# Half of the last stores issued from ScalarE's queue, with new due times for the planned order

## The chip, the cores and the metric

The kernel runs on one core of a Trainium2 chip. A core has a matrix engine (TensorE, PE in the profile), a vector engine (VectorE, DVE), a scalar engine for functions by table (ScalarE, ACT), GpSimd (POOL) and a sync engine (SyncE, SP), which here only issues DMAs. Each engine works through its own instructions in order; semaphores hold an instruction until what it needs is there. The metric is the device time of one execution in microseconds (us), the median of several runs.

## The reference, cut to what matters

The input u is 2048 positions by 512 channels. It is normalised, and the normalised xn goes two ways: through a long convolution whose kernel K comes from a state-space model with 128 states per channel, and through a mixing block with an MLP (512 to 1376 to 512).

```python
def reference(u, A_re, A_im, B_re, B_im, C_re, C_im, log_dt, Dskip, w1, w2, w3, w4):
    xn = layernorm(u)
    # K[d, l] = Re sum_n C[d, n] * exp(dt * A[d, n] * l) * dt * B[d, n]
    K = einsum("dn,dnl,dn->dl", C, exp(dt * A[:, :, None] * l), dt * B).real
    s = irfft(rfft(xn, 2L) * rfft(K, 2L))[:L] + xn * Dskip      # causal convolution
    h = gelu(layernorm(xn) @ w1)
    hs = shift_quarters(h, (+1, -1, +2, -2)) @ w2               # four channel quarters shifted in position
    x1 = xn + hs
    b = x1 + gelu(layernorm(x1) @ w3) @ w4
    return u + s * silu(b)
```

## The kernel before, in words

Positions lie on the 128 partitions in four quarters r of 32, with 16 slabs s of 512 channels; X, of 128 x 16 x 512, holds xn, then x1, then b, then the result. The convolution is done by hand-written Fourier steps as matrix products: u_stage1 transforms xn, tables(0) and tables(1) make K for two channel halves (phases, sines, cosines and exponentials on ScalarE and VectorE, sums on TensorE), kstage1 transforms K, products multiplies the spectra and starts the way back, and inverse ends it. The results of the stages go through DRAM (scr_Ud, scr_Kfa, scr_Zda and the like). mlp(g), for eight groups g of two slabs, is the largest part of TensorE's work: for each of six column blocks jp, 24 products into pb (fewer in the last block), a GELU on ScalarE, a split into two f16 parts (ghl), and 12 products into pa.

The end of the kernel, on which the change bears, is this. gate(g) applies SiLU to two slabs of X once mlp(g) is done. inverse(hf, g) (lines 898 to 911) loads zin from scr_Zda (hf = 0, the first 256 channels) or scr_Zdb (hf = 1, the second 256), does 8 small products per slab (pc or pd), and VectorE multiplies them into X. finish_first(g) (line 914) adds u to the first half of two slabs (the tile xh) and stores it; finish(g) (line 924) adds u to the second half (the tile xr, loaded for two groups at once) and stores it. A store goes by by_r (line 581): one DMA of 32 partitions, 64 KB, for each of the four quarters r. So each of the 16 calls issues four stores, 64 in all, and all of them from SP, which also issues every load and every store of the kernel.

The program order is not the order of execution. Every instruction is first put down in a Plan (line 147) with its dependencies, a cost, and a due time vt. Plan.order (line 253) then walks through time: it takes the engine that can start first, and of the operations that are ready there the one with the smallest vt. For an operation that ScalarE or VectorE may do (class Either), whichever engine comes first by these rules takes it, with a penalty added to vt (PREFER and AVOID, or PREFERP and AVOIDP where the source is in PSUM); a change of ScalarE's function table adds SWITCH. Operations on SP have a cost of 0.45 us, and their data lands later by a rate and the constant LAND. Each engine's instructions are then issued in that order. The vt of a step is set by due (line 575): a base, worked out from constants such as H0, MC, FA or FB, plus one entry of SHIFT for each of 361 calls. All instructions are issued from line 313, so the profile shows that line for nearly everything, and groups are told apart by the names of their tiles.

Of the kernel before, what the change touches and what calls it, by code (L numbers as in the profile page):

```python
# [83 lines left out]
class Op:  # L84
# [10 lines left out]
SAME = {"PE": 0.0, "ACT": 0.13, "DVE": 0.1, "SP": 0.0}  # L95
TABLE_LOAD = 1.41
DMA_RATE = 300e3
LAND, PAD = 2.65, 0.16
BASE, FINE, END = 16512, 19840, 229368

KGC, QUAD = 3.25, 0.95
WARM = 40

SHIFT = (
# [24 lines left out]
)  # L129
Q0, QC = -3744.9, 0.33  # L130
SWITCH = 12134.9
PREFERP, AVOIDP = 8082.45, -17238.7
PREFER, AVOID = 17860.0, 18183.0
PV, T0, TC = 1856.7, 239.9, 2383.42
LX, LC, LP, LW, LV = -4000.0, 0.08, -3071.8, 12710.4, 25366.6
M0, MC, WC = 1389.9, 9549.57, 0.4
H0, HC, SC = 4574.5, 2.54, 0.26
KA, PA, PAC, FA = -2867.9, -39190.2, 0.07, 17550.1
KB, PB, PBC, FB = 5280.7, 10111.3, 0.23, -6058.6
FC = 0.08  # L140


def mlp_due(g, jp):
# [3 lines left out]
class Plan:  # L147
# [105 lines left out]
    def order(self):  # L253
# [17 lines left out]
        while len(out) < len(ops):  # L271
# [4 lines left out]
            for o in pools[e]:  # L276
                if o.ready <= t + 0.02:
                    v = o.vt
                    if e == "ACT" and o.table and o.table != table:
                        v += SWITCH  # L280
                    if len(o.alts) > 1:
# [37 lines left out]
def is_ap(x):  # L319
    return hasattr(x, "tensor") and hasattr(x, "ap")  # L320


def columns(ap):
    n = 1
    for s in ap.shape[1:]:
        n *= s
    return n


def pe_cost(name, args):  # L330
    f = 1 if args[2].dtype == F16 else 4
    return 0.11 if name == "transpose" else columns(args[2]) * f / 2400.0 + 0.0025 * (1 + f // 4)


def act_cost(args, kw):
    small = sum(1 for k in ("bias", "scale") if is_ap(kw.get(k)))
    cost = columns(args[0]) * (0.00075 if "PSUM" in str(args[1].space) else 0.00084) + 0.092 + 0.088 * small
    return cost + (0.11 if is_ap(kw.get("accum_out")) else 0.0)


def dve_cost(name, args):
    aps = [a for a in args if is_ap(a)]
    n = columns(aps[0])
    small = sum(1 for a in aps[1:] if columns(a) == 1 and n > 1)
    if name == "bn_aggr":
        return 0.095
    if name == "reciprocal":
        return 0.07 + n * 0.0064
    if name == "memset":
        return 0.06 + n * 0.0003  # L350
    if name in ("bn_stats", "tensor_reduce"):
        return 0.045 + columns(aps[1]) / 960.0
    if name in ("tensor_scalar", "tensor_copy") and "PSUM" not in str(aps[1].space):
        return 0.068 + n * 0.00052 + 0.052 * small
    return 0.065 + n / 960.0 + 0.06 * small


class Engine:
# [3 lines left out]
    def __getattr__(self, name):  # L362
        def call(*args, **kw):
            aps = [a for a in args if is_ap(a)] + [kw[k] for k in ("bias", "scale") if is_ap(kw.get(k))]
            writes, reads = aps[:1], aps[1:]
            if is_ap(kw.get("accum_out")):
                writes = writes + [kw["accum_out"]]
            if name == "matmul" and not kw["start"]:
                reads = reads + writes
            table, nbytes = 0, 0  # L370
            if self.eng == "PE":
                cost = pe_cost(name, args)
            elif self.eng == "ACT":
                cost = act_cost(args, kw)
                if name == "activation":
                    table = TABLES.get(args[2], 0)
            elif self.eng == "DVE":
                cost = dve_cost(name, args)
            else:
                cost = 0.45  # L380
                nbytes = 4 * min(columns(a) * a.shape[0] for a in aps)
            self.plan.add({self.eng: (cost, (name, args, kw))}, writes, reads, table, nbytes)

        return call
# [38 lines left out]
def kernel(  # L423
# [9 lines left out]
    V, A, T, Q = [Engine(plan, e) for e in ("DVE", "ACT", "PE", "SP")]  # L433
# [3 lines left out]
    ov = out[0].rearrange("(t r s) d -> r t s d", r=4, s=S)  # L437
# [5 lines left out]
    DH = D // 2  # L443
# [13 lines left out]
    def at(offset, shape, dt, name):  # L457
        return nc.alloc_sbuf_tensor_at(name, shape, dt, offset=offset)[:]
# [116 lines left out]
    def due(t=None):  # L575
        plan.stage += 1
        t = plan.base = plan.base if t is None else t
        plan.vt = t + (SHIFT[plan.stage] if plan.stage < len(SHIFT) else 0)


    def by_r(sb, dr, to_dram=False):

        for r in range(4):
            a, d = sb[32 * r : 32 * r + 32], dr[r]
            Q.dma_start(d, a) if to_dram else Q.dma_start(a, d)

    w1s, w2s = [], []

# [304 lines left out]
    def gate(g):  # L893
        due(FA + FC * g)
        X2 = X[:, 2 * g : 2 * g + 2]
        A.activation(X2, X2, AF.Silu)

    def inverse(hf, g):
        due((FA, FB)[hf] + FC * g)
        ch = slice(hf * DH, hf * DH + DH)  # L900
# [13 lines left out]
    def finish_first(g):  # L914
        due(FA + FC * g)
        x = xhr([P, 2, DH], F32, "xh")
        by_r(x, xv[:, :, 2 * g : 2 * g + 2, :DH])
        X2 = X[:, 2 * g : 2 * g + 2, :DH]
        V.tensor_add(X2, X2, x)
        by_r(X2, ov[:, :, 2 * g : 2 * g + 2, :DH], to_dram=True)  # L920
# [3 lines left out]
    def finish(g):  # L924
        due(FB + FC * g)
        if g % 2 == 0:
            xr.append(at(xrs.pop(), [P, 4, DH], F32, "xr"))
            by_r(xr[-1], xv[:, :, 2 * g : 2 * g + 4, DH:])
        X2 = X[:, 2 * g : 2 * g + 2, DH:]
        V.tensor_add(X2, X2, xr[-1][:, 2 * (g % 2) : 2 * (g % 2) + 2])  # L930
        by_r(X2, ov[:, :, 2 * g : 2 * g + 2, DH:], to_dram=True)


    def pow2_scale(cols, dst_s, dst_inv, target):
# [301 lines left out]
    for g in range(8):  # L1236
        finish(g)
# [27 lines left out]
```

## Time and profile before

| | us |
|---|---|
| runs shown | 679.21, 679.72, 677.94 |
| median | 679.21 |
| profiled execution, its own time | 675.68 |
| its span, first to last instruction | 673.9 |
| mean granted TensorE clock | 0.969 |
| TensorE products busy | 629.6 |
| VectorE busy | 538.8 |
| ScalarE busy | 477.3 |
| 64 stores of the output, first issue to end of the last | 635.40 to 671.50 |

The profile shows one execution. Its engines are listed with their busy time; SPq is the queue of DMAs that SP issues, and the duration of a row there is that of the issue, not of the transfer. A row of the groups ends with the idle time of the engine just before it and what that time waited for. In the order of time each row has its start and its duration in us from the span's start.

### The profile page before, as it was taken

What the parts mean: (1) busy time and instruction counts of PE and PEld (TensorE: products, weight loads), DVE (VectorE), ACT (ScalarE), POOL (GpSimd) and SP (SyncE); (2) the same over time, 40 slices, a digit from 0 to 9 for tenths busy, and PEclk for the clock granted to TensorE, in tenths of its full rate; (3) what the DMA queues carried; (4) which work ended last, traced back from release to release, by engine and by line L of the source; (5) the groups of instructions that cost most, each with busy time, mean ns of one, the idle gap of its engine ahead of it and who ended that gap; (6) DMA issues with size and microseconds to landing.
All of it is one profiled execution on the core that took longest, in us unless ns stands there. A gap on an engine that the chain in (4) does not pass through costs nothing.

```text
span 673.9 us, 13919 instructions
## 1 busy us (share of the span) xinstructions
PE 629.6 (93%) x5526; PEld 417.0 (62%) x5526; DVE 538.8 (80%) x798; ACT 477.3 (71%) x1051; POOL 0.7 (0%) x6
## 2 busy tenths in 40 slices
PE   7799899999996998998999999999999999999972
PEld 7567667475465786565677576677555854567520
DVE  5899899999999999988999999987533247454472
ACT  3999899978877999896999996984534335242420
POOL 0000000000000000000000000000000000000000
PEclk9899979999998999998999999999999999999995
DMA  8945351511112110486233333343988778747954
GB/s 244 232 154 187 107 196 57 199 49 48 63 48 79 43 50 28 101 211 182 74 110 116 89 120 116 103 142 111 242 218 252 182 181 231 189 138 206 311 144 125
DMA packets 108432, 95.61 MB, mean 142 GB/s; under 512 B 49680, under 2 KB 90640, under 8 KB 107984
## 3 DMA queue, kind: packets, MB, share of 16 engines
q1 hardware_dynamic: 108368, 94.74, 49.8%
q8 instruction: 43, 0.70, 0.4%
q14 instruction: 21, 0.17, 0.1%
HBM read 61.16 MB, written 33.55 MB: 141 GB/s over the span
## 4 chain that ended last, share of the span: by engine, by line
PE 45%; DVE 36%; ACT 5%; DMA 5%; issue 4%; SPq 3%; DVEq 0%; ACTq 0%
PE pb L313 18%; DVE pt L313 11%; PE pa L313 10%; PE pc L313 9%; PE pd L313 8%; DVE kt L313 6%; DVE X L313 3%; SPq L313 3%; DVE pr L313 3%; DMA X<-in_A_u_dram 2%; DVE stats L313 2%; DVE eg L313 2%; ACT mag L313 2%; DVE ghl L313 2%; DVE pab L313 2%
## 5 line engine op out<-in xcount | busy, mean ns | idle before, releaser
L313 PE MATMUL pb<-x1T,w3h 128*128 128x256 f16 (+1 forms) x1056 | 125.2, 275 | 1.9 <-DVE w3h L313 1.0
L313 PE MATMUL pa<-w4h,ghl 128*128 128x512 f16 (+1 forms) x528 | 124.5, 384 | 1.2 <-DVE w4h L313 0.8
L313 PEld LDWEIGHTS <-w3h 128*128 128x128 f16 (+1 forms) x1056 | 102.6, 101 | 29.9 <-issue 15.2
L313 ACT ACT_TABLE_LOAD x78 | 100.1, 1283 | 2.4 <-PEq L1253 0.7
L313 PEld LDWEIGHTS <-ghl 128*128 128x128 f16 (+1 forms) x528 | 49.3, 99 | 67.8 <-issue 17.4
L313 ACT ACTIVATE mag<-par 128x64 f32<-128x64 f32 x512 | 85.2, 275 | 4.6 <-DVE kt L313 2.8
L313 PE MATMUL pc<-kt 128*32 128x64 f32 x1024 | 83.9, 417 | 0.6 <-DVE kt L313 0.6
L313 PE MATMUL pc<-pt 128*32 128x64 f32 x1024 | 77.6, 388 | 0.0
L313 PE MATMUL pb<-xT,w 128*128 128x256 f32 x256 | 61.3, 396 | 1.7 <-ACT hT L313 1.7
L313 PEld LDWEIGHTS pb<-xT,w 128*128 128x128 f32 x256 | 49.7, 198 | 14.2 <-issue 4.0
L313 PEld LDWEIGHTS pc<-pt 128*32 128x32 f32 x1024 | 55.9, 195 | 0.0
L313 ACT ACTIVATE g<-pb,wsc 128x512 f32<-128x512 f32 (+1 forms) x48 | 32.4, 690 | 32.5 <-PE pb L313 32.1
L313 PEld LDWEIGHTS pc<-kt 128*32 128x32 f32 x1024 | 48.3, 176 | 10.4 <-issue 7.5
L313 DVE SCALAR_TENSOR_TENSOR ghl<-g,wsc,ghl 128x512 f16<-128x512 f32 (+1 forms) x48 | 35.1, 739 | 24.4 <-ACT ghl L313 24.3
L313 DVE TENSOR_TENSOR kt<-mag,kt 128x1024 f32<-128x1024 f32 x32 | 42.8, 1336 | 0.3 <-ACT mag L313 0.3
L313 ACT ACTIVATE ghl<-g,wsc 128x512 f16<-128x512 f32 (+1 forms) x33 | 23.3, 710 | 24.6 <-PE pa L313 23.6
L313 DVE TENSOR_TENSOR pr<-pc,kh 128x512 f32<-128x512 f32 x32 | 21.0, 686 | 23.5 <-PE pc L313 17.1
L313 DVE SCALAR_TENSOR_TENSOR pt<-kt,pt 128x2080 f32<-128x2080 f32 x16 | 39.5, 2472 | 0.1
L313 PE MATMUL pd<-pr,cst 64*128 64x256 f32 x256 | 36.3, 402 | 1.1 <-DVE pr L313 1.1
L313 ACT COPY z1e<-pd 128x256 f32<-128x256 f32 x45 | 15.3, 383 | 29.2 <-PE pd L313 28.9
L313 ACT ACTIVATE kt<-kt,halfpi 128x2080 f32<-128x2080 f32 x16 | 32.3, 2020 | 0.0
L313 ACT ACTIVATE pt<-pt 128x2080 f32<-128x2080 f32 x16 | 31.3, 1959 | 0.1
(160 smaller groups left out, 970.3 us busy)
## 6 DMA issues: line engine op xcount, KB each, us to landing
wst<-in_B_w_dram SPq DMA_DIRECT2D x20, 512.0 KB, 3.7
scr_Ud<-ue SPq DMA_DIRECT2D x16, 512.0 KB, 3.2
scr_Kfa<-k1e SPq DMA_DIRECT2D x16, 256.0 KB, 3.5
uin<-scr_Ud SPq DMA_DIRECT2D x32, 128.0 KB, 2.9
cst<-c_gp SPq DMA_DIRECT2D x16, 256.0 KB, 2.8
kin<-scr_Kfa SPq DMA_DIRECT2D x32, 128.0 KB, 2.7
scr_Zda<-z1e SPq DMA_DIRECT2D x16, 256.0 KB, 2.7
cst<-c_gp SPq DMA_DIRECT2D x8, 512.0 KB, 4.2
```

Source lines behind the costliest of these rows:

```text
L313: ins = [getattr(self.engines[op.eng], name)(*args, **kw).ins for name, args, kw in op.calls]
```

## The change

Two edits of the code, and new numbers. by_r takes a pair of queues and uses them in turn for stores; finish passes SP's and ScalarE's, so that quarters 0 and 2 of each second half are stored from SP and quarters 1 and 3 from ScalarE. finish_first still stores from SP alone, and all loads stay on SP. The planner counts 0.45 us for a DMA on ScalarE. All 361 entries of SHIFT, the constants of the bases, the penalties and LAND (2.65 to 2.66) are replaced, so the planned order changes throughout.

```diff
-LAND, PAD = 2.65, 0.16
+LAND, PAD = 2.66, 0.16
 SHIFT = (
...
 )
-Q0, QC = -3744.9, 0.33
-SWITCH = 12134.9
-PREFERP, AVOIDP = 8082.45, -17238.7
-PREFER, AVOID = 17860.0, 18183.0
-PV, T0, TC = 1856.7, 239.9, 2383.42
-LX, LC, LP, LW, LV = -4000.0, 0.08, -3071.8, 12710.4, 25366.6
-M0, MC, WC = 1389.9, 9549.57, 0.4
-H0, HC, SC = 4574.5, 2.54, 0.26
-KA, PA, PAC, FA = -2867.9, -39190.2, 0.07, 17550.1
-KB, PB, PBC, FB = 5280.7, 10111.3, 0.23, -6058.6
-FC = 0.08
+Q0, QC = -11967.6, 0.09
+SWITCH = 10650.5
+PREFERP, AVOIDP = 13121.6, -24212.5
+PREFER, AVOID = 25936.6, 18011.2
+PV, T0, TC = 6435.1, 7692.7, 2695.8
+LX, LC, LP, LW, LV = -4000.0, 0.48, -17943.2, -1849.6, 49755.3
+M0, MC, WC = 10270.3, 8551.58, 0.66
+H0, HC, SC = 12245.0, 0.07, 0.14
+KA, PA, PAC, FA = -19279.1, -38345.8, 0.43, 41121.5
+KB, PB, PBC, FB = 3161.8, 3594.7, 0.05, -41595.5
+FC = 0.06
...
             elif self.eng == "ACT":
-                cost = act_cost(args, kw)
+                cost = 0.45 if name == "dma_start" else act_cost(args, kw)
...
-    def by_r(sb, dr, to_dram=False):
+    def by_r(sb, dr, to_dram=False, queues=(Q, Q)):
 
         for r in range(4):
             a, d = sb[32 * r : 32 * r + 32], dr[r]
-            Q.dma_start(d, a) if to_dram else Q.dma_start(a, d)
+            queues[r % 2].dma_start(d, a) if to_dram else Q.dma_start(a, d)
...
-        by_r(X2, ov[:, :, 2 * g : 2 * g + 2, DH:], to_dram=True)
+        by_r(X2, ov[:, :, 2 * g : 2 * g + 2, DH:], to_dram=True, queues=(Q, A))
```

49 rows, old and new, of the table SHIFT are left out of this document.

## The prediction

> **What bounds the kernel now.** I read the page first, then busy times in five stretches, then the order of time and the chain of waits over the last 40 us, then the groups of that tail and of the middle.
>
> ```profile
> span 673.9 us, 13919 instructions
> PE 629.6 (93%) x5526; PEld 417.0 (62%) x5526; DVE 538.8 (80%) x798; ACT 477.3 (71%) x1051; POOL 0.7 (0%) x6
> PEclk9899979999998999998999999999999999999995
> ```
>
> TensorE is busy for 629.6 of 673.9 us, so 44 us are to be had at most without touching its work. The next view, whose columns are the stretch, its length, the busy time of each engine, the granted clock, the DMA share and GB/s, says where they lie.
>
> ```profile
> 0.00:40.00 40.00, 31.64 (x171) 26.59 (x172) 29.79 (x98) 26.51 (x79) 0.70 (x6) 0.91 0.94 245
> 40.00:120.00 80.00, 75.25 (x604) 57.62 (x603) 76.55 (x95) 76.37 (x182) 0.00 (x0) 0.96 0.40 132
> 120.00:400.00 280.00, 266.66 (x2454) 175.08 (x2455) 274.47 (x345) 249.12 (x565) 0.00 (x0) 0.98 0.32 93
> 400.00:650.00 250.00, 248.64 (x2207) 155.67 (x2204) 146.26 (x240) 124.26 (x227) 0.00 (x0) 1.00 0.67 184
> 650.00:674.00 24.00, 7.44 (x99) 2.08 (x97) 11.76 (x25) 1.06 (x1) 0.00 (x0) 0.63 0.49 126
> ```
>
> TensorE idles 8.4 us in the loads at the start, 4.8 us up to 120, 13.3 us from 120 to 400, 1.4 us from 400 to 650, and 16.6 us behind 650. From 120 to 400 VectorE is busy for 98% of the time and is the bound; from 400 to 650 TensorE is. Behind 650 no compute engine is: even VectorE works for only half of it. What ends last there is seen in the order of time (start, duration, engine, operation).
>
> ```profile
> 611.71 0.69 DVE L313 TENSOR_TENSOR X<-X,xh 128x512 f32<-128x512 f32 x1
> ...
> 628.04 0.69 DVE L313 TENSOR_TENSOR X<-X,xh 128x512 f32<-128x512 f32 x1
> ...
> 635.40 36.09 SPq L313 DMA_DIRECT2D out_dram<-X  x64
> ...
> 646.75 0.69 DVE L313 TENSOR_TENSOR X<-X,xr 128x512 f32<-128x512 f32 x1
> ...
> 648.50 0.66 PE L313 MATMUL pd<-zin,is 64*32 64x256 f32 x16
> ...
> 649.10 1.47 PE L313 MATMUL pa<-w4h,ghl 96*128 96x512 f16 x6
> ...
> 652.75 1.06 ACT L313 ACTIVATE X<-X 128x1024 f32<-128x1024 f32 x1 [8.04 <-DVE X L313]
> ...
> 660.60 1.43 PE L313 MATMUL pc<-zin,is 64*32 64x256 f32 x16 [0.56 <-DVE X L313]
> ...
> 660.91 0.69 DVE L313 TENSOR_TENSOR X<-X,xr 128x512 f32<-128x512 f32 x1
> ...
> 662.90 0.69 DVE L313 TENSOR_TENSOR X<-X,xr 128x512 f32<-128x512 f32 x1
> 670.58 0.92 SPq L313 DMA_DIRECT2D out_dram<-X  x2
> ```
>
> The last addition, which finishes the output, ends at 662.90 + 0.69 = 663.59. SP issues its last two stores until 670.58 + 0.92 = 671.50, and the span ends 2.4 us later. So for 7.9 us everything is computed and SP alone works off a queue. The chain of waits names the same thing (start, duration, what).
>
> ```profile
> 643.36 0.43 SPq L313
> 643.79 0.04 issue
> 643.83 0.44 SPq L313
> ...
> 648.16 1.59 SPq L313
> 649.75 0.04 issue
> 649.79 0.43 SPq L313
> ```
>
> One store costs 0.43 to 0.44 us and a gap of 0.04, 0.48 in all, and from 643.36 SP no longer waits for data. One issue took 1.59, 1.15 more than the others. (671.50 - 643.36 - 1.15) / 0.48 = 56, so 56 of the 64 stores stand in that train. They stand there because they were late: six additions of the first halves (the rows from 611.71 to 628.04) were done before the first store left at 635.40, so 24 stores were waiting already.
>
> **The change part by part.** *The stores.* Of the 64 stores, the 32 of the second halves are split: rows r = 1 and 3 of each group go to ScalarE's queue, two of the four, so 16 leave SP. The 32 of the first halves stay on SP.
>
> ```profile
> L313 DVE TENSOR_TENSOR X<-X,xr 128x512 f32<-128x512 f32 x8 | 5.5, 690 | 0.2
> L313 DVE TENSOR_TENSOR X<-X,xh 128x512 f32<-128x512 f32 x2 | 1.4, 686 | 0.0
> L313 DVE TENSOR_TENSOR X<-X,pc 128x256 f32<-128x256 f32 x10 | 3.8, 417 | 1.6 <-PE pc L313 1.5
> L313 PE MATMUL pc<-zin,is 64*32 64x256 f32 x80 | 6.0, 534 | 4.0 <-DVE X L313 4.0
> L313 PE MATMUL pd<-zin,is 64*32 64x256 f32 x64 | 3.0, 385 | 0.6 <-DVE X L313 0.6
> ```
>
> These groups are of the time after 644. All eight additions of second halves (xr) fall there, so all 16 stores that leave SP leave the train. In the old order SP would then hold 56 - 16 = 40 stores: 643.36 + 40 x 0.48 + 1.15 = 663.7. But the last group's two SP stores can't start before its addition ends: 663.59 + 0.05 + 2 x 0.48 = 664.6. That is the later of the two, so it holds. The gain is 671.50 - 664.6 = 6.9 us.
>
> What of it lies on ScalarE: 16 issues by 0.48 are 7.7 us. ScalarE's last work is the SiLU at 652.75, behind 8.04 us of idling, and nothing follows until 673.9; that is the cover. Queued behind a store that waits for its addition there is only this SiLU of the last slabs, and further stores; without the cover (stores ahead of a GELU of the last matrix products) each group of two would hold ScalarE for up to one period of the additions, 2.0 us between the last ones. The price of a store on ScalarE's queue isn't in this trace. The nearest rows are the same stores on SP:
>
> ```profile
> L313 SPq DMA_DIRECT2D out_dram<-X x64: 315/431/1864, 635.4 to 671.1; - x64
> DMA to landing us min/median/max: 1.7/1.7/5.5
> ```
>
> At the least, 0.32 us, ScalarE is through before SP and nothing changes. At the most, 1.86 us, 16 stores take 29.8 us, and from the first possible one (647.4, the end of the first second-half addition) ScalarE would issue until 677.2: 5.7 us worse than before. I take 0.48, the median with its gap, since the transfer is the same one.
>
> Would the transfers keep up? These rows are of the stretch before the train is alone, and of the train's end:
>
> ```profile
> 620.00:650.00 30.00, 30.00 (x267) 15.97 (x264) 14.40 (x27) 10.83 (x14) 0.00 (x0) 1.00 0.89 251
> 664.00:674.00 10.00, 0.00 (x0) 0.00 (x0) 0.00 (x0) 0.00 (x0) 0.00 (x0) 0.50 0.45 115
> ```
>
> 56 stores of 65.5 KB in 21.2 us (643.4 to 664.6) are 173 GB/s, where 251 have been moved. There is room.
>
> *The due times.* Every SHIFT and nearly every base changes, so the whole order does, though no instruction beside table loads is added or removed. In planning units the new values look like the old ones stretched by about half, with noise. Two readings of them: the second halves' steps now start from -41,595 and the first halves' from 41,122 (before: -6,059 and 17,550), so where both are ready the second halves go first, and the very last stores may be those that SP issues alone (four by 0.48, so 1.0 us later than in my sum). The penalty that keeps a free choice off VectorE rises from 17,860 to 25,937, that for ScalarE falls a little. Bounds of the reordering: all idle time of 120 to 400 gained, -13.3 us; as much again lost, +13.3. No row speaks for a sign, so I take 0.
>
> *The sum.* 673.9 - 6.9 = 667.0 span. The profiled execution took 675.68, 1.8 around its span, so 668.8 for such a run. The median of the runs, 679.21 (677.94 to 679.72), lies 3.5 above the profiled one; I keep that distance: 679.21 - 6.9 = 672.3.
>
> **The rivals.**
>
> *The tail shrinks further (668.9).* Once SP isn't last, the inverse steps are. After 644 there are nine of them (80 and 64 products, 16 in each), six of them behind the last matrix products of 649.10; at a clock of 0.63 one takes up to 1.43 us, where that at 648.50 took 0.66. If five of them go ahead of the last matrix products, those end 5 x 0.66 = 3.3 later, at 653.9. Then follow the two slabs' updates and the SiLU (3.2, as from 650.57 to 653.81), four multiplications by 0.417 and two additions by 0.69 (3.1), two stores (1.0) and 2.4: 663.6 span, 3.4 below my sum. For it speaks the dip of the clock in the last slice; against it that the 24 waiting stores must then leave before 635, or SP (663.7 + 2.4 = 666.1) is the bound again.
>
> *The two queues take turns (679.2).* The trace has no second queue, so it can't exclude that issuing is one resource. If a part t of each 0.48 is exclusive, the train ends at 643.36 + 56 t + 1.15, which passes 664.6 from t = 0.36 on; at t = 0.48 nothing is gained. For it: the shortest issue took 0.32, close to that point. Against it: the usual 0.43 stands for one queue alone, where the sequencer's own work is included.
> The Trainium skill, Perfetto Trace Analysis, section "DMA Instruction — HWDGE (DVE, Sync)", says that the descriptor generator is locked for one instruction while its descriptors are made, and that the sequencers share it; by that rule this rival has its place. The Trainium skill, DMA: Bandwidth & Descriptors, section "Issuing engines are not separate DMA queues", says that issuing on several engines saves just the sequencer's time to start a transfer; by that rule the full 6.9 stands, because here it is this time that is queued, and no run so far shows which page decides.
>
> *ScalarE overruns the middle (685.4): slower.* The rows are of 120 to 400.
>
> ```profile
> L313 DVE TENSOR_SCALAR kt<-pt 128x2080 f32<-128x2080 f32 (+1 forms) x9 | 12.1, 1346 | 0.1
> L313 ACT ACTIVATE kt<-pt,magic 128x2080 f32<-128x2080 f32 x5 | 10.1, 2022 | 1.7 <-DVE pt L313 1.6
> L313 ACT ACT_TABLE_LOAD x44 | 56.5, 1283 | 1.1 <-PE pb L313 0.4
> ```
>
> Nine phase steps that either engine may take run on VectorE at 1.35 us; on ScalarE the like takes 2.02. With the new penalties all nine may move: 18.2 us more on ScalarE, of whose 280 us 30.9 are free. The cost of changing its table falls from 12,135 to 10,651, so there may also be more table loads, at 1.28 each; ten fill what is left. From 17 more on (18.2 + 21.8 - 30.9 = 9.1) the loss passes the gain of 6.9 and the 2.0 us of a measurable difference; at 20 it is 13.0, and the time 679.2 - 6.9 + 13.0, 685.3 to 685.4. For it: 44 loads in 280 us are many already, and ScalarE is 89% busy. Against it: VectorE, the bound there, would be relieved by 12 us at the same time.
>
> *Part is given back (677).* The same stretch loses 3 to 7 us without a single cause.
>
> **How the numbers follow.** What a measurement of this kernel can tell from no change is about 0.3%, 2.0 us. My forecast, the stores' gain with an order that is worth the same, has 0.50 (its own range 669 to 675.5); the shorter tail 0.20; part given back 0.10, half of it within 2 us of the old time; the queues taking turns 0.06; the overrun 0.14. Faster: 0.50 + 0.20 + 0.05 = 0.75; the same: 0.05 + 0.06 = 0.11; slower: 0.14. The range 666.5 to 680.5 leaves out the overrun and the best of the shorter tails; it takes in half of the reordering's gain and no more than the old time with a little on top.
>
> **What would show it.** Right, if the profile after has 16 stores on ScalarE's queue and 48 on SP's, the last SP issue ends within about 1.5 us of the last addition instead of 7.9 behind it, the stores on ScalarE take 0.3 to 0.6 us, and the stretch behind the last matrix product falls from 23 to about 16 us. The queues take turns if issues on both stretch to 0.8 us and more where they overlap. The overrun shows as more than 60 table loads between 120 and 400 and as ScalarE busy throughout a stretch in which TensorE idles. Wrong I am if TensorE's idle time between 40 and 650, 19.5 us now, changes by more than 5 us either way, or if the span's end is set by something else than a store.

## The result and the profile after

The changed kernel takes 673.88 us (median of four runs, 672.62 to 674.53), where the kernel before took 678.92 beside it (677.94 to 679.72). The ratio is 0.9924, with a 95% interval of 0.9904 to 0.9944. Measured again later, beside the kernel before, it was 675.31 against 679.36 (0.9941, 0.9913 to 0.9968). So it is 4 to 5 us faster. The forecast was 672.3. The way there is another one than forecast, as the rest shows.

The first lines of the profile after: the span, the engines' busy time and the granted clock.

```profile
span 672.1 us, 13936 instructions
PE 630.7 (94%) x5526; PEld 418.5 (62%) x5526; DVE 535.1 (80%) x788; ACT 479.2 (71%) x1060; POOL 0.7 (0%) x6
PEclk9889979999997998999999999999999999999995
```

The span is 1.8 us shorter, and the profiled execution took 673.90. Its stretches, with the columns of the table before (stretch, length, the engines, clock, DMA share, GB/s):

```profile
0.00:40.00 40.00, 31.13 (x167) 26.20 (x168) 30.31 (x100) 26.37 (x79) 0.70 (x6) 0.87 0.90 242
40.00:120.00 80.00, 75.86 (x610) 58.98 (x609) 75.57 (x92) 76.90 (x184) 0.00 (x0) 0.96 0.40 133
120.00:400.00 280.00, 266.58 (x2422) 175.52 (x2421) 275.29 (x341) 254.35 (x596) 0.00 (x0) 0.97 0.33 94
400.00:650.00 250.00, 249.21 (x2238) 155.62 (x2236) 142.56 (x235) 120.51 (x204) 0.00 (x0) 1.00 0.65 183
650.00:674.00 24.00, 7.94 (x96) 2.15 (x96) 11.38 (x24) 1.06 (x1) 0.00 (x0) 0.61 0.51 133
```

Up to 650 the two kernels look alike: TensorE idles 4.1 + 13.4 + 0.8 = 18.4 us between 40 and 650, where it was 19.5. What is new stands in the tail. First the stores by queue (shortest, median and longest issue in ns; first and last start):

```profile
L314 SPq DMA_DIRECT2D out_dram<-X x48: 315/426/1961, 633.2 to 669.3; - x48
L314 ACTq DMA_DIRECT2D out_dram<-X x16: 322/437/460, 647.7 to 664.1; - x16
...
DMA to landing us min/median/max: 1.6/1.7/5.0
```

Then the order of time of the tail (start, duration, engine, operation):

```profile
643.50 26.24 SPq L314 DMA_DIRECT2D out_dram<-X  x36
...
646.08 2.77 PE L314 MATMUL pa<-w4h,ghl 128*128 128x512 f16 x12
...
647.02 0.69 DVE L314 TENSOR_TENSOR X<-X,xr 128x512 f32<-128x512 f32 x1
647.75 0.87 ACTq L314 DMA_DIRECT2D out_dram<-X  x2
...
652.96 11.57 ACTq L314 DMA_DIRECT2D out_dram<-X  x14
...
662.88 0.69 DVE L314 TENSOR_TENSOR X<-X,xr 128x512 f32<-128x512 f32 x1
```

The last addition ends at 662.88 + 0.69 = 663.57, as before (663.59). SP's last issue ends at 643.50 + 26.24 = 669.74, 6.2 us behind it, where it was 7.9. So SP still works alone at the end, with 16 stores fewer: its 36 last stores take 26.24 us, and at 0.48 each they would take 17.3. The waits of SP's queue over the tail, and the piece of the chain of waits in which the longest of them stands, tell where most of these 9 us went (total, times, longest; then start, duration, what):

```profile
SPq L314 <- DMA out_dram<-X: 8.7, 5, 4.9
```

```profile
647.02 0.70 DVE X L314
647.72 0.02 issue
647.75 1.69 DMA out_dram<-X
649.44 0.02 issue
649.46 0.32 SPq L314
```

Before, SP had no such wait. Here ScalarE issues its first store at 647.75, once the addition is done; the store lands at 649.44; and 0.02 us later SP issues a store of its own, which has nothing to do with that data. SP stood still for that from 644.5 on, 5.0 us, though stores of first halves were ready.

Why it waits is seen in the built program. The framework has eight completion semaphores for DMAs and hands them out in turn, over both queues in one list, in the planned order. A DMA that is given a semaphore is issued only when the DMA that had it before, eight places earlier in the list, has landed. The built program shows it for all of its 428 DMAs from the ninth on, and the trace shows it here: SP's store at 649.46 waits for the same semaphore that ScalarE's store of 647.75 counts up. As long as all stores stand on SP, that is a store which SP itself issued long ago. With ScalarE's stores in the list, eight places earlier may stand a store that ScalarE can't issue yet, because its addition isn't done; then SP stands still, and all that is queued behind it.

### The profile page after: what moved, and what is told of

It reads as the page before. It is cut to its first block, busy times and chain, and to the rows that moved or that the text cites. A ratio compares the mean times of both kernels' runs of the same rounds, so it can differ in the third digit from the quotient of the medians.

```text
span 672.1 us, 13936 instructions
## 1 busy us (share of the span) xinstructions
PE 630.7 (94%) x5526; PEld 418.5 (62%) x5526; DVE 535.1 (80%) x788; ACT 479.2 (71%) x1060; POOL 0.7 (0%) x6
## 4 chain that ended last, share of the span: by engine, by line
PE 49%; DVE 34%; ACT 5%; issue 4%; DMA 4%; SPq 1%; DVEq 0%; ACTq 0%
PE pb L314 17%; PE pa L314 14%; DVE pt L314 12%; PE pd L314 11%; PE pc L314 8%; DVE kt L314 7%; DVE X L314 3%; DMA X<-in_A_u_dram 2%; DVE stats L314 2%; DVE pr L314 2%; ACT kt L314 2%; DVE eg L314 2%; DVE pab L314 2%; SPq L314 1%; ACT L314 1%
## 5 line engine op out<-in xcount | busy, mean ns | idle before, releaser
L314 PE MATMUL pb<-x1T,w3h 128*128 128x256 f16 (+1 forms) x1056 | 127.4, 278 | 0.5 <-ACT g L314 0.5
L314 PE MATMUL pa<-w4h,ghl 128*128 128x512 f16 (+1 forms) x528 | 122.2, 381 | 2.0 <-ACT ghl L314 1.3
L314 ACT ACTIVATE ghl<-g,wsc 128x512 f16<-128x512 f32 (+1 forms) x43 | 30.1, 713 | 20.0 <-PE pa L314 19.8
L314 DVE TENSOR_TENSOR kt<-mag,kt 128x1024 f32<-128x1024 f32 x32 | 40.7, 1273 | 0.0
L314 DVE TENSOR_TENSOR pr<-pc,kh 128x512 f32<-128x512 f32 x32 | 20.8, 686 | 19.5 <-PE pc L314 10.9
L314 ACT ACTIVATE kt<-kt,halfpi 128x2080 f32<-128x2080 f32 x16 | 33.8, 2115 | 0.0
L314 ACT COPY z1e<-pd 128x256 f32<-128x256 f32 x37 | 12.9, 382 | 28.5 <-PE pd L314 27.1
```

The source lines that it names most:

```text
L314: ins = [getattr(self.engines[op.eng], name)(*args, **kw).ins for name, args, kw in op.calls]
```

## The experiments

The theory from this profile: **the split alone gains nothing, because SP waits for ScalarE's stores through the shared list; most of the gain is the due times'.** The first rival is the forecast's reading, that the split is worth 6.9 and the new order loses some of it again. The second is that stores cost more when two queues issue them.

**Each half of the change alone.** *split_only* has the two edits of the code with the old due times, constants and LAND; *due_only* has the new numbers with all stores on SP.

```diff
-        by_r(X2, ov[:, :, 2 * g : 2 * g + 2, DH:], to_dram=True, queues=(Q, A))
+        by_r(X2, ov[:, :, 2 * g : 2 * g + 2, DH:], to_dram=True)
```

> The old due times with 16 of the second halves' stores on ScalarE's queue, nothing else. My prediction's sum (SP's train just gets shorter by 16 stores): 6.9 us less, span about 667.0, median about 672. The theory that I form from the profile after (a store on SP waits until the store eight places ahead of it in the common list of both queues has landed, and the list puts ScalarE's late stores ahead of SP's ready ones): SP stands still from about 645 to 649.2 and again until about 663.3, then has some 19 stores left, so the last issue ends near 672.4 and the span is about 675, no gain (between -2 and +2 us against before). Rival, the queues take turns at issuing: issues on SP stretch from 0.48 to 0.8 us and more wherever ScalarE issues too, no waits of several us, span about 674.

> The new due times with all stores on SP. The prediction's sum (split worth 6.9, due times worth 0): as before, median 679. The waiting theory (the split gains nothing in the new order because its 7.7 us of standing still eat the 16 stores): as after or within 1.5 us of it: 52 stores from 643.5 on by 0.48 and 0.8 extra end at 669.3, span about 671.7, median 673 to 675; SP waits for no store. The whole measured gain of 5.0 us would then be the due times'. Rival, the queues take turns: the same as after as well, so this run tells the share of the due times, not the cause.

Measured: *split_only* 680.54 (12 runs, 678.42 to 683.51), ratio 1.0024 (1.0005 to 1.0043); *due_only* 675.50 (6 runs), ratio 0.9942 (0.9919 to 0.9965), against the same runs of the kernel before, 678.80. SP's waits, its stores and the last addition in *split_only*, and then SP's stores and the last addition in *due_only*:

```profile
SPq L313 <- DMA out_dram<-X: 10.9, 6, 5.2
```

```profile
639.32 37.37 SPq L313 DMA_DIRECT2D out_dram<-X  x48
...
667.04 0.69 DVE L313 TENSOR_TENSOR X<-X,xr 128x512 f32<-128x512 f32 x1
```

```profile
635.31 9.16 SPq L314 DMA_DIRECT2D out_dram<-X  x12
645.00 26.94 SPq L314 DMA_DIRECT2D out_dram<-X  x52
...
664.51 0.69 DVE L314 TENSOR_TENSOR X<-X,xr 128x512 f32<-128x512 f32 x1
```

With the split alone SP stands still for 10.9 us and ends at 676.69, 9.0 us behind the last addition: more than before. The split alone makes the kernel no faster, by its ratio 1.6 us slower. The new due times alone make it 3.9 us faster (0.0058 of 679); the 675.50 lies 0.5 above the 673 to 675 expected. The whole change gained 5.2 when first measured and 4.0 when measured again, by its ratios, so 0.1 to 1.2 us are left for the split in it, which these intervals can't tell from nothing.

**The wait taken away.** *lanes* is the changed kernel with one edge of dependency more for each of ScalarE's 16 stores: it also waits until a certain one of SP's stores has been issued. Work and queues stay the same, and an added edge can only hold ScalarE longer; but it moves ScalarE's stores back in the common list, behind SP stores that are ready before them (in the built program the first of them goes from place 373 to place 385 of 428).

```diff
+            if op.calls[0][0] == "dma_start" and "out_0" in op.calls[0][1][0].tensor.name:
+                if op.eng == "SP":
+                    stored.append(op)
+                else:
+                    tc.add_manual_dep(op.first, stored[behind.pop(0)].last.name, info, reason="place among the stores")
```

with `behind = [16, 17, 28, 29, 30, 31, 32, 33, 36, 37, 39, 40, 42, 43, 44, 45]`, the place of that store among SP's 48.

> The kernel after, but each store on ScalarE also waits for one of SP's stores (numbers 16, 17, 28 to 33, 36, 37, 39, 40, 42 to 45 of SP's 48) that should have landed by then: this moves ScalarE's stores back in the common list, so that SP's ready stores no longer stand eight places behind a late one. Waiting theory: SP's standing still (8.7 us in after) falls under 1.5 us, SP's last issue ends near 664.7 to 665.5, span 667 to 668, median 669 to 670, 4 to 5 us below after. Rival, the queues take turns or the transfers limit the train: no gain, span 671 to 673, with SP's issues stretched. If the added waits are late themselves, ScalarE's last stores end last and the span lies between.

Measured: 670.83 (6 runs, 667.98 to 671.57), ratio 0.9865 (0.9840 to 0.9890), measured beside the two kernels above. SP's waits and the order of time:

```profile
SPq L315 <- DVE X L315: 3.5, 6, 1.1
...
SPq L315 <- DMA out_dram<-X: 0.2, 1, 0.2
```

```profile
645.10 21.36 SPq L315 DMA_DIRECT2D out_dram<-X  x36
...
656.08 10.47 ACTq L315 DMA_DIRECT2D out_dram<-X  x14
...
664.95 0.69 DVE L315 TENSOR_TENSOR X<-X,xr 128x512 f32<-128x512 f32 x1
```

The wait for stores falls from 8.7 to 0.2 us. SP now waits for additions, as it should, and its last issue ends at 666.46, 0.8 behind the last addition. The result is 4.7 us below *due_only*, which has the same due times and no second queue (670.83 against 675.50): the split does have its worth, once it brings no wait. The time is 0.8 above the 669 to 670 expected. In the profile SP's end is 1.0 above the 664.7 to 665.5 expected, while the last addition, at 665.64, ends 2.1 later than in after.

**The same with the old due times**, beside the kernel before and the changed kernel with profiles of their own: *split_lanes* is *split_only* with such edges (`behind = [12, 13, 17, 18, 23, 24, 25, 26, 31, 32, 36, 37, 41, 42, 43, 44]`); *before_again* and *after_again* are the two kernels unchanged.

> The old due times, 16 stores on ScalarE's queue, and each of these also behind one of SP's stores (numbers 12, 13, 17, 18, 23 to 26, 31, 32, 36, 37, 41 to 44 of SP's 48), so that none of SP's ready stores stands eight places behind a late one. Waiting theory: SP's last issue now ends about 1 us behind the last addition instead of 7.5 to 9, as the prediction's sum had it: 5.5 to 7 us below before, median 672 to 673.5; the split is worth what I predicted, once the waits are gone. Rival, that the new due times are needed for any gain: within 1.5 us of before.

> The kernel before once more, for its profile: the one on record took 675.68 us, 2.3 below the lowest and 3.5 below the median of the runs, while the profile after (673.90) lies on its median. If that profile was an unusually short execution, this one has a span of 676 to 677.5, and the rows that are longer say where executions differ. If executions with a profile are shorter for this kernel, it has about 674 again.

> The kernel after, on the same chip as the others here: 4 to 6 us below before, as first measured (673.88 against 678.92). Its profile shows how far the start varies: TensorE's idle time in the first 40 us was 8.4 to 13.3 in the profiles so far, and I expect the last addition, less that time, at 653 to 655 here and in due_only and lanes, and at 655 to 657 with the old due times.

Measured: *split_lanes* 674.01 (6 runs), ratio 0.9920 (0.9890 to 0.9950), the kernel before 679.36 beside it; *after_again* 675.31 (9 runs). Its wait for stores is there again, 8.4 us. The last addition, less TensorE's idle time in the first 40 us, was expected at 653 to 655 with the new due times and at 655 to 657 with the old; it is at 652.3 to 655.4 (*after*, *after_again*, *due_only*, *lanes*, *lanes_again*) and at 655.2 to 657.5 (*before*, *before_again*, *split_only*, *split_lanes*), so the order is right and the bounds are too narrow. The stores and the last addition of *before_again*, then SP's wait, the stores and the last addition of *split_lanes*:

```profile
639.02 35.81 SPq L313 DMA_DIRECT2D out_dram<-X  x64
...
666.69 0.69 DVE L313 TENSOR_TENSOR X<-X,xr 128x512 f32<-128x512 f32 x1
```

```profile
SPq L314 <- DMA out_dram<-X: 1.5, 2, 1.1
```

```profile
638.77 29.34 SPq L314 DMA_DIRECT2D out_dram<-X  x48
...
658.04 10.40 ACTq L314 DMA_DIRECT2D out_dram<-X  x12
...
666.60 0.69 DVE L314 TENSOR_TENSOR X<-X,xr 128x512 f32<-128x512 f32 x1
```

Here the last additions end within 0.1 us of each other, and SP ends at 674.83 and at 668.11: 6.7 us earlier, where 6.9 was forecast for the split. ScalarE's last store ends at 668.44, so all stores together end 6.4 earlier. In the medians it is 5.4 (679.36 - 674.01), just under the 5.5 to 7 expected.

**What is last next.** In *lanes* the last four additions come 1.98 to 1.99 us apart, one per inverse step, because the last steps all use the same pair of PSUM banks and each waits for the multiplications of the step before. *banks* is *lanes* with the last ten inverse steps taking the two pairs in turn, in the planned order as it was. In it the multiplications of one step read the products of a later one, so a part of the output is computed from these; instructions and sizes are the same.

> The kernel lanes, in which the last ten inverse steps use the PSUM pairs pd and pc in turn, where pc had come five times running; planned order and everything else unchanged. In lanes the last additions come every 1.98 us: TensorE's 1.53 and VectorE's first multiplication of 0.41 take turns on one pair. If the pair is what holds them, the period falls to about 1.5 (VectorE's 1.44 of work each), the last addition comes about 2.4 us earlier, and SP, which has work until about 664 to 665 in lanes' time, takes back about half: 1 to 2.4 us below lanes (670.83), median 668.5 to 670. If the period is TensorE's start or its clock, it stays at 1.98 and the time with it.

Measured: 670.20 (6 runs), ratio 0.9861 (0.9825 to 0.9898), the same as *lanes*, where 1 to 2.4 us less was expected. The last additions come 1.39 us apart (662.71, 664.10), and the last one ends at 664.79; but ScalarE's last store only at 667.91, 3.1 us behind it, and the span's end comes 5.5 behind it. So the stores took back what the steps had gained; the edges were those chosen for *lanes*, but which wait held these stores wasn't settled. *banks2* changes the 14th and the 16th step alone, where each multiplication still has its own products, and lets the edges follow:

```diff
+        self.pairs = {}
...
+                    turn[k] = ("pd" in op.calls[0][1][0].tensor.name) != (len(turn) in (13, 15))
...
-        stored, behind = [], [16, 17, 28, 29, 30, 31, 32, 33, 36, 37, 39, 40, 42, 43, 44, 45]
+        stored, behind = [], [16, 17, 28, 29, 30, 31, 32, 33, 35, 36, 37, 38, 39, 40, 41, 42]
```

> As the kernel with the added waits, but the 14th and the 16th inverse step take the other pair of PSUM banks, so that the last inverse steps alternate between two pairs, where they all took one pair and each waited for the multiplications of the step before. Theory: with the stores no longer standing still, the last inverse steps are the bound of the tail; the period of the last additions falls from about 2.0 to about 1.4 us for two or three of them, the last addition comes 1 to 1.5 us earlier, and the time is 1 to 1.5 us below the kernel with the added waits. Rival: the stores are the bound still; the last addition comes earlier, the last store doesn't, and the time stays the same within 0.5 us.

> The kernel with the added waits of ScalarE's stores, once more in the same call as the next one: 670 to 672 as before. Both theories expect the same of it; it is the base for the next kernel.

Measured: *banks2* 668.98 (6 runs, 667.70 to 672.73), ratio 0.9848 (0.9821 to 0.9875); *lanes_again* 671.85 (6 runs, 668.76 to 675.13), ratio 0.9890 (0.9861 to 0.9920). The additions of *lanes_again*, and those and the stores of *banks2*:

```profile
651.04 0.68 DVE L315 TENSOR_TENSOR X<-X,xr 128x512 f32<-128x512 f32 x1
...
660.74 0.69 DVE L315 TENSOR_TENSOR X<-X,xr 128x512 f32<-128x512 f32 x1
...
662.73 0.69 DVE L315 TENSOR_TENSOR X<-X,xr 128x512 f32<-128x512 f32 x1
```

```profile
648.76 19.54 SPq L320 DMA_DIRECT2D out_dram<-X  x36
...
656.30 0.68 DVE L320 TENSOR_TENSOR X<-X,xr 128x512 f32<-128x512 f32 x1
...
665.25 0.69 DVE L320 TENSOR_TENSOR X<-X,xr 128x512 f32<-128x512 f32 x1
666.63 0.69 DVE L320 TENSOR_TENSOR X<-X,xr 128x512 f32<-128x512 f32 x1
```

From the addition at 651.04 to the last one it is 11.69 us in *lanes_again*; from its counterpart at 656.30 it is 10.33 in *banks2*, 1.4 us less, and SP's last issue ends 1.0 behind it (668.30 against 667.32). That is what was expected of the tail. The medians differ by 2.9, but the two intervals overlap, so the trace's 1.4 is the better figure. By its median *banks2* is the best version: by the ratios of the two, 0.9% (0.9848 against 0.9941) or 0.8% (against 0.9924) below the changed kernel, and 1.5% below the kernel before.

## Why the prediction was right, and where it wasn't

The time is right, 673.88 against 672.3 with a range of 666.5 to 680.5, but by luck: errors cancel. The split was to bring 6.9 us and the due times nothing; in the whole change the split brought 0.1 to 1.2, and the due times 3.9. The sum shows it too. The span was forecast at 667.0 and is 672.1, 5.1 too little. From the span to the median 5.3 us were added (1.8 around the span, and 3.5 because the median stood above the profiled execution); in the kernel after it is 1.8. 5.1 - 3.5 = 1.6, the difference that is left.

- **What bounds the tail**: right. The due times alone leave 6.7 us of stores behind the last addition (671.94 against 665.20), and in *split_lanes* and *lanes* the end came forward with SP's train.
- **16 stores leave SP, and SP issues two stores behind the last addition (664.6)**: the count is right, the end is not. In after, SP ends at 669.74, 5.1 later than that sum. The step that failed is "from 643.36 SP no longer waits for data", carried over to the changed kernel. It was true of one queue; with two, the list of completion semaphores ties one to the other, and 8.7 us of waiting came in. That the wait is the cause isn't argued only: with 10.9 us of it the split was worth nothing (*split_only*), and with 1.5 us of it, at the same due times, SP's last store came 6.7 us earlier than in the kernel before (*split_lanes* against *before_again*), where the sum had 6.9.
- **0.48 for a store on ScalarE's queue**: right, from bounds of 0.32 to 1.86. The median issue is 437 ns, with the gap 0.48.
- **The due times at nothing**: wrong, they are worth 3.9 us, inside the bounds of 13.3 but most of the gain. Where they come from is found only in part. The spans of *before_again* and *due_only* differ by 2.9 us. Of that, 2.2 is an earlier last addition (665.20 against 667.38), which isn't placed further. From 280 to 320 TensorE's idle time falls from 2.5 us to 0.2 (the rows are of *before_again* and *due_only*, the first with a wait of 2.0 for a load of uin where the second has one of 0.2), but from 120 to 280 and from 320 to 400 it idles 2.9 us longer, so that stretch can't be named as the place of the gain:

```profile
280.00:320.00 40.00, 37.47 (x385) 22.57 (x381) 35.33 (x44) 32.18 (x81) 0.00 (x0) 0.96 0.63 166
```

```profile
280.00:320.00 40.00, 39.78 (x451) 26.72 (x449) 39.06 (x41) 39.49 (x104) 0.00 (x0) 1.00 0.68 187
```

  The other 0.7 lies behind the last addition: SP ends 6.7 behind it instead of 7.5 in *before_again* (674.83 against 667.38). In *due_only* 12 stores are out before the train begins (64 - 52), where it was 8 in the profile of before. The remaining 1.0 of the 3.9 stands in the medians alone.
- **The distance of 3.5 from the profiled execution to the median**: wrong to keep it. The profile of before was a quick execution: TensorE idled 8.4 us in its first 40, where it idled 11.4 in *before_again*, whose span is 677.2, 3.3 longer.
- **The queues take turns**: refuted. Between 652.96 and 655.4 of after both issue at once:

```profile
652.96 2.34 ACTq L314 DMA_DIRECT2D out_dram<-X  x5
...
653.00 2.41 SPq L314 DMA_DIRECT2D out_dram<-X  x5
```

  Five issues each in 2.34 and 2.41 us are 0.47 and 0.48 for one, the price of a queue alone. The Trainium skill, DMA: Bandwidth & Descriptors, section "Issuing engines are not separate DMA queues", by which issuing on two engines saves the sequencer's time, agrees with these rows; the lock of the shared generator, which the Trainium skill, Perfetto Trace Analysis, section "DMA Instruction — HWDGE (DVE, Sync)", describes for DVE and Sync, costs nothing here between SP and ScalarE that a row shows.
- **ScalarE overruns the middle**: refuted. In after there are 40 table loads from 120 to 400, four fewer, and ScalarE is busy for 254 of the 280 us.
- **Part is given back**: by the spans 5.1 us of the 6.9 are missing, but in the tail, by SP's waits, and not, as the rival had it, from 120 to 400, where TensorE's idle time went from 13.3 to 13.4 us.
- **The tail shrinks further**: not in after, whose last additions come as late as before. The point it made, that the inverse steps are last once SP isn't, holds in *lanes*, and *banks2* takes 1.4 us of it.

Of the signs that the prediction named, two failed: the last issue came 6.2 us behind the last addition and not within 1.5, and from the end of the last products into pa (646.08 + 2.77 = 648.85) to the span's end (672.1) it is still 23.3 us. These two alone show, beside a time that came out well, that the reason was wrong.

## What to carry to other kernels

Before stores are moved to a second queue, look at what the two queues share: completion semaphores handed out in turn tie a queue whose data is ready to one whose data is late, and here 8.7 us of such waiting left next to nothing of a gain of 6.9. Put the late transfers behind the ready ones in the order in which the semaphores are handed out (an added edge was enough, 4.7 us), and read the waits of a queue for a DMA of the other. A time that agrees with a forecast doesn't confirm its reason: change one half at a time.

## What the runs showed that was not expected

- Two queues issue side by side without slowing each other: five 64 KB stores in 2.34 us on ScalarE's and five in 2.41 on SP's at the same time, and a store of after lands 1.7 us after its issue (median), as it did on one queue (up to 1.9 in the other kernels with two queues).
- Executions of one kernel differ by how the loads of the start come in: in the profile of before twelve 256 KB loads of u landed 6.8 us after their issue (median) and TensorE was busy for 31.64 us of the first 40; in *before_again* it was 9.3 and 28.58, and the spans differ by 3.3 us. So two spans are to be compared from a point behind the start, or by medians.
- In after, at a granted clock of 0.61 behind 650, the 16 small products of an inverse step take 1.43 us where they took 0.66 at 648.77, and a period of the last additions is 1.98 us with one pair of PSUM banks (*lanes*) and 1.39 with two (*banks*).
